# Turning softmax weights by block transposes and a trip through DRAM instead of TensorE transposes, from the tenth head pair on

## The chip, the cores and the metric

One core of a Trainium2 chip runs the kernel. The metric is device time in microseconds (us) of one execution; a version's figure is the median of several runs. One further execution was taken with the profiler, and its rows are what the text argues from.

## The reference

Three parts follow one another, all in float32: sliding-window attention, and two feed-forward layers whose input is the attention's output.

```python
scores = scale * q @ k^T                          # B=4, H=8, S=576, D=64
scores = where((rel >= 0) & (rel < 128), scores - slope_h * |rel|, -1e9)
attn = exp(scores - max); attn = attn / (sum + 1e-9)
x = (attn @ v), heads side by side                # 2304 tokens x 512
h = x @ w_in                                      # 512 x 2048
x = (h * clip(h + 3, 0, 6) / 6) @ w_out
xn = x / sqrt(mean(x*x) + 1e-6) * rms_g
out = (silu(xn @ w_gate) * (xn @ w_val)) @ w_out  # 512 x 1536
```

## The kernel before

The 2304 tokens are 18 tiles of 128, handled in six blocks of three (`BLOCKS`). The program is written out in the order in which each engine is to work; nothing reorders it. Its spine is a row of **slots**. A slot takes one of the 16 chunks of the first layer's hidden width (`m`) for one block: `product1` (L463, 12 matmuls of 384 columns into the single bank `ps_h`), then an activation chain on ScalarE and VectorE that makes `g` from `ps_h` (L699 relu, L700 product, L705 and L711 its high and low part), and `product2` (L476, 9 matmuls of 512 columns) of the slot before, whose `g` is ready. The next slot's `product1` needs `ps_h` free again, which L700 does; `product2` one slot on needs `g`.

Attention is threaded into these slots. A **pair** is two heads of one block: 24 pairs, each of three **steps** (one tile of 128 queries each, against the keys of that tile and the one before). The list `slots` says in which slot each kind of work of a step is done: S scores (L341), the bias, the row's minimum and the exponentials (L355, L362, L370, then the reciprocal on GpSimd, L372 and L373); D the division by the sum (L378); T or L two transposes on TensorE (L384) into the bank `turned_bank`, a copy back to SBUF (L389) and, where the two key tiles were folded into one by a minimum (`joint`, from the tenth pair on), two `affine_select` on GpSimd that unfold them (L391); V the product with the values (L402). From block 2 on a pair begins every four slots, at `m % 4 == 2`, with the plan S (0, 0, 0), D (1, 1, 2), T (-, 2, 3), L (1, -, -), V (5, 5, 5): slots after the pair's first, for its three steps. So the four slots of a cycle are unlike each other: one with the scores, one with the values of the pair before, and two without either.

Beside this run, all issued from one DMA queue (SP) in program order: loads of keys, queries and values (L295, L297, L302); from slot `m = 2` of block 2 on the conversion of the second layer's 36 weight pieces (`Second`: load L202, `begin` and `turn` on VectorE and ScalarE, stores L224 and L230); and `Norm`, which squares, scales and block-transposes three tiles per block (L505, L513, L530) and stores them with four DMAs of 512 runs of 128 bytes each (L520), a run being 32 float32. The last block's 16 slots have no attention, and the second layer follows (L824, L876).

Of the kernel before, what the change touches and what calls it, by code (L numbers as in the profile page):

```python
# [10 lines left out]
F32 = mybir.dt.float32  # L11
# [3 lines left out]
U64 = mybir.dt.uint64  # L15
AF = mybir.ActivationFunctionType
ALU = mybir.AluOpType
# [43 lines left out]
EARLY = {0: 1, 1: 3, 2: 6, 3: 8, M2 - 1: 11}  # L61
PAIRS2 = NTILE // 6

KINDS = "QSDTLV"

OPEN = {"reuse_waits": "tile"}

# [1 line left out]
def f32(ap):  # L69
    return ap.bitcast(F32)  # L70
# [3 lines left out]
def fused_kernel(ctx: ExitStack, tc: tile.TileContext, qd, kd, v, w1, w2, rms_g, out):  # L74
# [113 lines left out]
    class Second:  # L188
# [2 lines left out]

        def __init__(self):
            self.n, self.loaded, self.done, self.raw, self.run = 3 * M2, 0, 0, [], None
            self.whole = [dram.tile([P, 4, HK], F32, tag=f"b_{m}", name=f"b_{m}") for m in range(M2)]
            self.parts = [dram.tile([P, 2, 7, HK], F32, tag=f"t_{m}", name=f"t_{m}") for m in range(M2)]
            self.out = [dram.tile([P, 2, 2, DM], F32, tag=f"w2_{m}", name=f"w2_{m}") for m in range(M2 // 2)]

        def load(self):
            i = self.loaded
            if i < self.n:  # L200
                raw = wcpool.tile([P, DM], U64, tag="w", name="wraw", bufs=2)
                sp.dma_start(out=raw, in_=w2[i // 3, :, (i % 3) * DM : (i % 3 + 1) * DM])  # L202
                self.raw.append(raw)
                self.loaded += 1

        def begin(self):

            if self.raw:
                self.run = convert(self.raw.pop(0), DM, wcpool, 1, 3, vec)
                for _ in range(3):  # L210
                    next(self.run)

        def turn(self):

            if self.run is None:
                return
            i, self.done = self.done, self.done + 1
            m, kind = divmod(i, 3)
            run, self.run = self.run, None
            x = run.send(None)  # L220
            self.load()
            if kind < 2:
                self.begin()
                sp.dma_start(out=self.whole[m][:, kind::2], in_=x.rearrange("p (a k) -> p a k", a=2))  # L224
            else:
                t = wcpool.tile([P, 2, DM], F32R, tag="wt", name="w", bufs=1)
                run.send(t)
                self.begin()
                next(run)
                sp.dma_start(out=self.out[m // 2][:, m % 2], in_=f32(t))  # L230

    class Parts:

# [38 lines left out]
    att = ExitStack()  # L272
    ap = att.enter_context(tc.tile_pool(name="ap", bufs=3))
    xs_of = {}
    pairs_bank = [ps_a.tile([P, 2, 2 * P], F32, tag=f"S{a}", name=f"ps_s{a}") for a in range(2)]
    spare_bank = [ps_out.tile([P, 2 * P], F32, tag=f"o{a}", name=f"ps_s{a}") for a in range(2)]
    turned_bank = ps_a.tile([P, 2, 2, P], F32, tag="T", name="ps_t")
# [3 lines left out]
    class Pair:  # L281
# [25 lines left out]
        def scale(self):  # L307
            q = self.qr[:, : self.n * P]
            vec.tensor_scalar(q, q, qscale[:, self.j : self.j + 1], None, ALU.mult)

        def finish(self):

            nq = self.n * P
            x = self.acc.rearrange("p u q -> p (u q)")[:, :nq]
            if self.j == 0:
                xs = (x0pool if self.b == 0 else xpool).tile([P, KC, 2, 3 * P], F32R, tag="xs", name="xs")
                xs_of[self.b] = [xs[:, c] for c in range(KC)]
            t = xs_of[self.b][self.j]
            act.copy(t[:, 0, :nq], x)
            vec.tensor_sub(t[:, 1, :nq], x, f32(t[:, 0, :nq]))  # L320

    class Step:
# [51 lines left out]

        def divide(self):
            for a in range(2):
                p = self.t[:, a, self.p0 :]
                vec.tensor_scalar(p, p, self.r[:, a : a + 1], None, ALU.mult)  # L378

        def transpose(self):  # L380
            self.ps = turned_bank
            for a in range(2):
                for c in range(self.p0 // P, 2):
                    pe.transpose(self.ps[:, a, c], self.t[:, a, c * P : (c + 1) * P], ident)  # L384

        def weights(self):

            self.pt = ap.tile([P, 2, 2, P], F32, tag="pt", name="pt", bufs=3)
            act.copy(self.pt[:, :, self.p0 // P :], self.ps[:, :, self.p0 // P :])  # L389
            for c, sign in ((0, -1), (1, 1)) if self.joint else ():  # L390
                pool.affine_select(  # L391
                    out=self.pt[:, :, c], in_=self.pt[:, :, 1], compare_op=ALU.is_ge, fill=0.0,
                    base=c - 1, pattern=[[0, 2], [sign, P]], channel_multiplier=-sign,
                )

        def values(self):
            pr = self.pair
            if pr.acc is None:
                pr.acc = sums_bank[:, :3]
            for c in range(self.from_, 2):  # L400
                for a in range(2):
                    pe.matmul(  # L402
                        pr.acc[a * D : (a + 1) * D, self.u],
                        lhsT=pr.vr[:, self.i - 1 + c - pr.lo, a * D : (a + 1) * D],
                        rhs=self.pt[:, a, c],
                        start=(c == self.from_),
                        stop=(c == 1),
                        skip_group_check=True,
                    )
# [8 lines left out]
    for k, pr in enumerate(pairs):  # L418
        b, j = divmod(k, H // 2)
        if b < 2:  # L420
            t0, plan = 3 * j if b == 0 else AHEAD - 3 + 3 * j, {"S": (0, 1, 2), "D": (1, 2, 3), "T": (2, 3, 4), "V": (3, 4, 5)}
        else:
            t0, plan = AHEAD + M1 * (b - 1) - 2 + 4 * j, {"S": (0, 0, 0), "D": (1, 1, 2), "T": (None, 2, 3), "L": (1, None, None), "V": (5, 5, 5)}
        slots["Q"].setdefault(t0 - (2 if b < 2 else 1), []).append(pr)
        for u in range(pr.n):
            step = Step(pr, u)
            for kind, at in plan.items():
                if at[u] is not None:
                    slots[kind].setdefault(t0 + at[u], []).append(step)

# [123 lines left out]
    busy(WARM)  # L554
    pairs[0].scale()
    for t in range(AHEAD):
        q, s_, d_, t_, _, v_ = at(t)
# [104 lines left out]
    for p, (b, m0, m1) in enumerate(PARTS):  # L662
# [13 lines left out]
        xs = xs_of[b]  # L676
        for m in range(m0, m1):
            t, slot = slot, slot + 1
            q, s_, d_, t_, l_, v_ = at(t)
            go = p < 3 or last or (t - AHEAD) % 4 in (0, 3)  # L680
            if p == 3 and m == 2:
                first.close()
                wcpool = second.enter_context(tc.tile_pool(name="wcpool", bufs=1, side="right", **OPEN))
                W2.load()
                W2.load()
# [12 lines left out]
            r = gpool.tile([P, 3 * P], F32, tag="t", name="t", bufs=1)  # L698
            act.activation(r[:, :nq], ps[:, :nq], AF.Relu, bias=three)  # L699
            vec.scalar_tensor_tensor(out=r[:, :nq], in0=r[:, :nq], scalar=6.0, in1=ps[:, :nq], op0=ALU.min, op1=ALU.mult)  # L700
            for x in t_:
                x.weights()
            for x in d_:
                x.divide()
            act.copy(g[:, 0, :nq], r[:, :nq])  # L705
            for x in s_[:2]:
                x.bias()
# [8 lines left out]
            if go:  # L716
                for x in norms:
                    x.scale()
            prepare(q, s_)
            if pend:  # L720
                finish1(go)
            for x in l_:
                x.transpose()
            if p == 0:
                k = m + 1
                W1.load(k + 4)
# [17 lines left out]
            for x in norms:  # L744
                x.store()
            if last:
                if m == 1:
                    fed = Inputs(0)
# [240 lines left out]
```

## Time and profile before

| | |
|---|---|
| median of 3 runs | 943.26 us (942.93 to 944.92) |
| profiled execution | 944.16 us, of which the span in the profile is 942.4 us |
| granted TensorE clock, mean | 0.992 |
| TensorE matmul busy | 924.7 us, 98% |
| VectorE busy | 634.7 us, 67% |
| ScalarE busy | 444.9 us, 47% |
| GpSimd busy | 184.5 us, 20% |
| DMA | 97,242 packets, 175.05 MB |

The engines run side by side, so busy times don't add up. The chain that ended last is followed back from the last instruction: what stands in it set the end. The text below writes slots by their place in a pair's cycle: S slot (`m % 4 == 2`), then V slot, P slot and R slot, `m % 4` being 3, 0 and 1.

### The profile page before, as it was taken

What the parts mean: (1) busy time and instruction counts of PE and PEld (TensorE: products, weight loads), DVE (VectorE), ACT (ScalarE), POOL (GpSimd) and SP (SyncE); (2) the same over time, 40 slices, a digit from 0 to 9 for tenths busy, and PEclk for the clock granted to TensorE, in tenths of its full rate; (3) what the DMA queues carried; (4) which work ended last, traced back from release to release, by engine and by line L of the source; (5) the groups of instructions that cost most, each with busy time, mean ns of one, the idle gap of its engine ahead of it and who ended that gap; (6) DMA issues with size and microseconds to landing.
All of it is one profiled execution on the core that took longest, in us unless ns stands there. A gap on an engine that the chain in (4) does not pass through costs nothing.

```text
span 942.4 us, 14933 instructions
## 1 busy us (share of the span) xinstructions
PE 924.7 (98%) x5474; PEld 818.9 (87%) x5474; DVE 634.7 (67%) x1327; ACT 444.9 (47%) x949; POOL 184.5 (20%) x327
## 2 busy tenths in 40 slices
PE   7899999999999999999999999999999999999998
PEld 4577888888888888888898999999999999999997
DVE  5788667555878777876477567787545577545555
ACT  6899666455555655655455553433131323131120
POOL 4333112333223422422233214110000000000000
PEclk8899999999999999999999999999999999999999
DMA  6455501124776565554356759876757555755521
GB/s 231 177 208 192 193 21 49 34 55 121 200 232 197 164 180 171 178 141 150 123 184 240 290 196 317 288 261 233 253 213 271 202 201 201 268 207 208 208 103 68
DMA packets 97242, 175.05 MB, mean 186 GB/s; under 512 B 42768, under 2 KB 70672, under 8 KB 92816
## 3 DMA queue, kind: packets, MB, share of 16 engines
q1 hardware_dynamic: 97168, 174.09, 54.5%
q8 instruction: 43, 0.70, 0.3%
q14 instruction: 31, 0.25, 0.1%
HBM read 130.03 MB, written 44.04 MB: 185 GB/s over the span
## 4 chain that ended last, share of the span: by engine, by line
PE 85%; DVE 6%; ACT 5%; issue 2%; POOL 1%; DMA 0%; ACTq 0%; POOLq 0%; DVEq 0%
PE ps_o L476 18%; PE ps_h L463 18%; PE ps_y L876 15%; PE ps_o L824 10%; PE ps_S L824 8%; PE ps_A L824 6%; PE ps_h L824 4%; PE ps_av L402 3%; PE ps_t L384 2%; PE ps_s L341 2%; ACT wx L136 1%; DVE t L700 1%; ACT t L370 1%; DVE wx L143 1%; ACT w L145 1%
## 5 line engine op out<-in xcount | busy, mean ns | idle before, releaser
L476 PE MATMUL ps_o<-w,g 128*128 128x512 f32 x864 | 222.0, 401 | 3.3 <-ACT w L145 3.1
L463 PE MATMUL ps_h<-xs,w 128*128 128x384 f32 x1152 | 219.6, 338 | 0.1
L463 PEld LDWEIGHTS ps_h<-xs,w 128*128 128x128 f32 x1152 | 201.9, 188 | 8.6 <-DVE t L700 2.9
L476 PEld LDWEIGHTS ps_o<-w,g 128*128 128x128 f32 x864 | 156.1, 188 | 42.3 <-ACT w L145 5.9
L876 PE MATMUL ps_y<-wo,g 128*128 128x512 f32 (+1 forms) x654 | 150.0, 387 | 0.0
L876 PEld LDWEIGHTS ps_y<-wo,g 128*128 128x128 f32 x654 | 121.9, 188 | 24.0
L700 DVE SCALAR_TENSOR_TENSOR t<-t,ps_h 128x384 f32<-128x384 f32 x96 | 53.2, 554 | 93.8 <-ACT t L699 93.8
L699 ACT ACTIVATE t<-ps_h,three 128x384 f32<-128x384 f32 x96 | 55.3, 576 | 87.7 <-PE ps_h L463 85.6
L884 DVE TENSOR_TENSOR y<-y,ps_y 128x512 f32<-128x512 f32 (+1 forms) x91 | 61.9, 680 | 34.4 <-PE ps_y L876 33.9
L370 ACT ACTIVATE t<-t,m 128x128 f32<-128x128 f32 (+1 forms) x144 | 61.2, 426 | 29.4 <-DVE t L362 16.1
L705 ACT CAST g<-t 128x384 fp32r<-128x384 f32 x96 | 49.3, 514 | 48.7 <-DVE t L700 47.1
L711 DVE TENSOR_TENSOR g<-t,g 128x384 fp32r<-128x384 f32 x96 | 54.7, 570 | 23.0 <-ACT g L705 22.0
L847 ACT ACTIVATE r<-r 128x384 f32<-128x384 f32 x36 | 18.9, 525 | 103.0 <-DVE r L846 103.0
L824 PE MATMUL ps_o<-S,tw 128*128 128x384 f32 x336 | 66.2, 339 | 0.0
L372 POOL TENSOR_SCALAR r<-den 128x2 f32<-128x2 f32 x72 | 27.5, 383 | 185.4 <-ACT t L370 183.7
L824 PEld LDWEIGHTS ps_o<-S,tw 128*128 128x128 f32 x336 | 59.3, 188 | 1.0 <-DVE u L835 0.8
L373 POOL TENSOR_TENSOR r<-r,minus 128x2 f32<-128x2 f32 x72 | 56.0, 777 | 6.0
L391 POOL TENSOR_SCALAR_AFFINE_SELECT pt<-pt 128x256 f32<-128x256 f32 x82 | 34.9, 425 | 95.7 <-ACT pt L389 92.5
L832 ACT COPY s<-ps_S 128x384 f32<-128x384 f32 x18 | 8.6, 479 | 84.0 <-PE ps_S L824 83.9
L136 ACT ACTIVATE wx<-wraw 128x512 f32<-128x512 f32 (+1 forms) x52 | 42.6, 818 | 2.7 <-DMA wraw<-w 2.7
L143 DVE SCALAR_TENSOR_TENSOR wx<-wx,wy 128x512 uint32<-128x512 uint32 (+1 forms) x52 | 43.8, 843 | 0.0
L384 PE MATMUL ps_t<-ident,t 128*128 128x128 f32 x190 | 35.6, 292 | 8.1 <-DVE t L378 6.1
(136 smaller groups left out, 1450.4 us busy)
## 6 DMA issues: line engine op xcount, KB each, us to landing
tw<-t SPq DMA_DIRECT2D x52, 896.0 KB, 6.3
wraw<-w SPq DMA_DIRECT2D x36, 512.0 KB, 4.2
wo<-w SPq DMA_DIRECT2D x18, 1024.0 KB, 4.9
wraw<-w SPq DMA_DIRECT2D x16, 1024.0 KB, 8.5
t<-th SPq DMA_DIRECT2D x12, 896.0 KB, 4.6
t<-tl SPq DMA_DIRECT2D x12, 896.0 KB, 4.5
b<-wx SPq DMA_DIRECT2D x24, 256.0 KB, 3.0
w<-w SPq DMA_DIRECT2D x12, 512.0 KB, 3.2
```

The lines of the kernel that those rows point to most:

```text
L143: vec.scalar_tensor_tensor(out=xi, in0=xi, scalar=3, in1=y, op0=ALU.logical_shift_left, op1=ALU.bitwise_or)
L370: act.activation(p, p, AF.Exp, bias=self.m[:, a : a + 1], scale=-1.0, accum_out=self.den[:, a : a + 1])
L373: pool.tensor_tensor(self.r, self.r, minus, ALU.pow)
L384: pe.transpose(self.ps[:, a, c], self.t[:, a, c * P : (c + 1) * P], ident)
L463: pe.matmul(ps[:, : n * P], lhsT=w[:, a, c * P : (c + 1) * P], rhs=xs[c][:, b, : n * P], start=(k == 0), stop=(k == 3 * KC - 1),)
L476: pe.matmul(o, lhsT=g[:, a, i * P : (i + 1) * P], rhs=w[:, b], start=(m == first and a == 0 and b == 0), stop=(m == last and b == 1),)
L699: act.activation(r[:, :nq], ps[:, :nq], AF.Relu, bias=three)
L700: vec.scalar_tensor_tensor(out=r[:, :nq], in0=r[:, :nq], scalar=6.0, in1=ps[:, :nq], op0=ALU.min, op1=ALU.mult)
L711: vec.tensor_sub(g[:, 1, :nq], r[:, :nq], f32(g[:, 0, :nq]))
L824: pe.matmul(ps, lhsT=w[a][:, k, c * P : (c + 1) * P], rhs=x[:, b, c], start=(start and j == 0), stop=(j == 5), skip_group_check=True,)
L876: pe.matmul(ps[:, cols], lhsT=gs[i + k][:, a, t // 3, t % 3 * P : (t % 3 + 1) * P], rhs=wo[i + k][:, b, cols], start=(k == 0 and a == 0 an ...
L884: vec.tensor_add(acc[t][:, cols], acc[t][:, cols], ps[:, cols])
```

## The change

For the steps of the last 15 pairs (`via`; 45 steps) the weights are turned another way:

- The division moves to ScalarE (two activations with a scale per row, 128x128 each), one slot after the scores, behind `finish1`.
- In the next slot (P) VectorE transposes the step's 128x2x128 weights in blocks of 32x32 (`Step.turn`), and SP stores them to a DRAM tile (`Step.put`, 128 KB, runs of 512 bytes).
- One slot on (R) SP loads the pair's three steps back with four DMAs (`Pair.fetch`, 32 partitions each), which put the blocks at their turned places: 768 runs of 128 bytes per DMA, 3072 per pair.
- One slot on, GpSimd does the `affine_select`s for all three steps (W), and V stays five slots after S.

The 45 TensorE steps of transposing (90 instructions) and their 45 copies from PSUM go. Beyond that: `weights_` is one tile in place of the three `pt` buffers, its axes reordered; stores of converted weights are issued one slot later (`W2.flush`), and those of the norm in the slot after their transposes; a third buffer for the raw weights; the norm's work is done once in four slots (`m % 4 == 1`) rather than twice; and one unit of the first layer's conversion is begun at `m = 5` rather than 7.

```diff
-LAST_UNITS = {CUT: (1, 3, 4), CUT + 1: (4, 5, 7), CUT + 2: (7, 8, 9), CUT + 3: (9, 11, 12)}
+LAST_UNITS = {CUT: (1, 3, 4), CUT + 1: (4, 5, 7), CUT + 2: (5, 8, 9), CUT + 3: (9, 11, 12)}
...
-                raw = wcpool.tile([P, DM], U64, tag="w", name="wraw", bufs=2)
+                raw = wcpool.tile([P, DM], U64, tag="w", name="wraw", bufs=3)
...
+        def flush(self):
+            for out, x in self.stores:
+                sp.dma_start(out=out, in_=x)
+            self.stores = []
...
+        def fetch(self):
+
+            for k in range(0, P, 32):
+                sp.dma_start(
+                    out=weights_[k : k + 32, 1].rearrange("r u a (b s) -> r (u a b) s", s=32),
+                    in_=self.d[:, :, :, k : k + 32].rearrange("u a (b r) s -> r (u a b) s", r=32),
+                )
...
+            self.via = self.joint or self.c0 == P and pair.b * H // 2 + pair.j >= JOINT
+            self.pt = weights_[:, :, u]
...
-                p = self.t[:, a, self.p0 :]
-                vec.tensor_scalar(p, p, self.r[:, a : a + 1], None, ALU.mult)
+                p, r = self.t[:, a, self.p0 :], self.r[:, a : a + 1]
+                if self.via:
+                    act.activation(p, p, AF.Copy, scale=r)
+                else:
+                    vec.tensor_scalar(p, p, r, None, ALU.mult)
+
+        def turn(self):
+
+            vec.transpose(self.t[:, :, :P], self.t[:, :, P:])
+
+        def put(self):
+            if self.first:
+                self.pair.d = dram.tile([3, 2, P, P], F32, tag="pd", name="pd", bufs=2)
+            sp.dma_start(out=self.pair.d[self.u].rearrange("a p k -> p a k"), in_=self.t[:, :, :P])
...
+            steps = {"S": plan["S"], "D": (1, 1, 1), "P": (2, 2, 2), "R": (None, None, 3), "W": (4, 4, 4), "V": (5, 5, 5)} if step.via else plan
...
-            go = p < 3 or last or (t - AHEAD) % 4 in (0, 3)
+            go = p < 3 or last or m % 4 == 1
...
+            for x in w_:
+                x.select()
             ps = ps_h.tile([P, 4 * P], F32, tag="h", name="ps_h")
             product1(ps, W1.w_in(m), xs, n)
...
             vec.scalar_tensor_tensor(out=r[:, :nq], in0=r[:, :nq], scalar=6.0, in1=ps[:, :nq], op0=ALU.min, op1=ALU.mult)
+            for x in p_:
+                x.turn()
             for x in t_:
                 x.weights()
...
             prepare(q, s_)
+            W2.flush()
+            for x in norms:
+                x.store()
+            for x in p_:
+                x.put()
+            for x in r_:
+                x.pair.fetch()
             if pend:
                 finish1(go)
             for x in l_:
                 x.transpose()
+            for x in d_:
+                if x.via:
+                    x.divide()
```

How the instructions move shows in the order of each engine. First TensorE, in the V, P and R slots of a pair from block 2 on, before:

```order
L463 MATMUL ps_h<-xs,w 128x384 x12
L402 MATMUL ps_av<-pt,vraw 64x128 x12
L476 MATMUL ps_o<-w,g 128x512 x9
L384 MATMUL ps_t<-ident,t 128x128 x2
L463 MATMUL ps_h<-xs,w 128x384 x12
L384 MATMUL ps_t<-ident,t 128x128 x2
L476 MATMUL ps_o<-w,g 128x512 x9
L463 MATMUL ps_h<-xs,w 128x384 x12
L384 MATMUL ps_t<-ident,t 128x128 x2
```

and the same stretch of the change (its lines are some 30 higher):

```order
L496 MATMUL ps_h<-xs,w 128x384 x12
L434 MATMUL ps_av<-pt,vraw 64x128 x12
L509 MATMUL ps_o<-w,g 128x512 x9
L496 MATMUL ps_h<-xs,w 128x384 x12
L509 MATMUL ps_o<-w,g 128x512 x9
L496 MATMUL ps_h<-xs,w 128x384 x12
```

The three rows of two transposes are gone, and nothing takes their place on this engine. Second ScalarE, from a V slot to the P slot behind it, in the change:

```order
L734 ACTIVATE t<-ps_h,three 128x384
L743 CAST g<-t 128x384
L335 CAST xs<-ps_av 128x384
L397 ACTIVATE t<-t,r 128x128 x6
L145 CAST w<-wx 128x512
L136 ACTIVATE wx<-wraw 128x512
```

where the kernel before had, between L319 (there the `xs` cast) and the next relu:

```order
L319 CAST xs<-ps_av 128x384
L145 CAST w<-wx 128x512
L136 ACTIVATE wx<-wraw 128x512
L389 COPY pt<-ps_t 128x2x128
L699 ACTIVATE t<-ps_h,three 128x384
```

Six divisions came in ahead of the weight conversion, and the copies left. Third the DMA queue SP, one full cycle of the change from the keys' load in an S slot on:

```order
L303 DMA kraw<-kd 128x512
L305 DMA qraw<-qd 128x384
L216 DMA b_108<-wx 256x1x256
L553 DMA x_0_145<-y 32x16x32 x4
L203 DMA wraw<-w 128x512
L310 DMA vraw<-v 128x4x128
L216 DMA b_108<-wx 256x1x256
L203 DMA wraw<-w 128x512
L216 DMA w_1_130<-w 128x1024
L408 DMA pd<-t 128x2x128 x3
```

Behind them come `L203` (a load), `L216` (the store of the P slot's piece) and the four `L322` that fetch: the three stores of the weights stand behind one store of converted weights, and the fetch behind a load and a store.

## Rows read from the trace of the kernel before

**Rows 1.** The page: span, and part 1, busy time and share of each engine.
```profile
span 942.4 us, 14933 instructions
PE 924.7 (98%) x5474; PEld 818.9 (87%) x5474; DVE 634.7 (67%) x1327; ACT 444.9 (47%) x949; POOL 184.5 (20%) x327
```
**Rows 2.** The chain that ended last, 139 to 445 us: its shares by line.
```profile
by line: PE ps_o L476 39.6%; PE ps_h L463 38.8%; PE ps_av L402 6.0%; PE ps_t L384 3.3%; PE ps_s L341 3.3%; PE ps_t L341 1.3%; DMA wraw<-w 1.1%; DVE t L355 0.9%; ACT t L370 0.8%; DVE t L700 0.7%; ACT t L699 0.7%; issue 0.7%; ACT wx L136 0.6%
```
**Rows 3.** The same chain in time, one pair's cycle: start us, us, what.
```profile
362.18 2.11 PE ps_h L463 x12
...
367.70 2.11 PE ps_h L463 x12
...
373.54 0.22 PE ps_t L384 x2
373.76 2.09 PE ps_h L463 x12
375.85 0.22 PE ps_t L384 x2
376.07 2.06 PE ps_o L476 x9
...
380.24 0.22 PE ps_t L384 x2
...
382.52 2.11 PE ps_h L463 x12
```
**Rows 4.** The same chain, two slots without attention.
```profile
460.37 2.08 PE ps_o L476 x9
462.45 2.10 PE ps_h L463 x12
```
**Rows 5.** TensorE's waits, 139 to 445 us: us in total, times, longest.
```profile
PE ps_t L384 <- ACT pt L389: 0.5, 2, 0.3
```
**Rows 6.** Groups by line and shape: count | busy us, mean ns | idle before, releasers.
```profile
L370 ACT ACTIVATE t<-t,m 128x128 f32<-128x128 f32 x90 | 35.5, 395 | 21.5 <-DVE t L362 16.1 <-POOL r L372 5.5
L389 ACT COPY pt<-ps_t 128x256 f32<-128x256 f32 x45 | 16.4, 365 | 3.8 <-PE ps_t L384 3.6
L378 DVE TENSOR_SCALAR t<-t,r 128x128 f32<-128x128 f32 x98 | 23.0, 289 | 1.6 <-POOL r L373 1.5
L530 DVE STREAM_TRANSPOSE y<-y 128x512 f32<-128x512 f32 x18 | 12.7, 704 | 0.0
L391 POOL TENSOR_SCALAR_AFFINE_SELECT pt<-pt 128x256 f32<-128x256 f32 x82 | 34.9, 425 | 95.7 <-ACT pt L389 92.5
```
**Rows 7.** Timeline of that cycle, ScalarE: V slot into P slot.
```profile
371.89 0.47 ACT L319 CAST xs<-ps_av 128x384 fp32r<-128x384 f32 x1
374.05 0.62 ACT L145 CAST w<-wx 128x512 fp32r<-128x512 f32 x1 [1.69 <-DVE wx L143]
374.58 0.69 ACT L136 ACTIVATE wx<-wraw 128x512 f32<-128x512 f32 x1
...
375.95 0.58 ACT L699 ACTIVATE t<-ps_h,three 128x384 f32<-128x384 f32 x1 [0.42 <-PE ps_h L463]
```
**Rows 8.** The same timeline on GpSimd and VectorE.
```profile
370.77 0.70 POOL L373 TENSOR_TENSOR r<-r,minus 128x2 f32<-128x2 f32 x1
...
376.56 0.56 DVE L700 SCALAR_TENSOR_TENSOR t<-t,ps_h 128x384 f32<-128x384 f32 x1 [1.01 <-ACT t L699]
```
**Rows 9.** DMA from 213.0 to 215.4 us, one tile's four norm stores (128-byte runs).
```profile
DMA packets 2112, 0.26 MB, mean 109 GB/s; under 512 B 2112, under 2 KB 2112, under 8 KB 2112
q1 hardware_dynamic: 2112, 0.26, 68.6%
x<-y SPq DMA_DIRECT2D x3, 64.0 KB, 2.0
```
**Rows 10.** DMA from 169 to 171 us, one load of values (512-byte runs).
```profile
q1 hardware_dynamic: 528, 0.26, 43.6%
```
**Rows 11.** The page, part 6: issues, KB each, median us to landing.
```profile
b<-wx SPq DMA_DIRECT2D x24, 256.0 KB, 3.0
```
**Rows 12.** Busy us (count) of PE, PEld, DVE, ACT, POOL; clock, DMA share, GB/s.
```profile
360.00:380.00 20.00, 20.00 (x137) 17.40 (x137) 15.01 (x41) 11.51 (x31) 5.80 (x13) 1.00 0.50 164
```

More of the change, by code (lines that the diff above doesn't have):

```diff
@@ L62 @@
 PAIRS2 = NTILE // 6
-KINDS = "QSDTLV"
+KINDS = "QSDTLVPRW"
 OPEN = {"reuse_waits": "tile"}
@@ L211, in begin @@
                     next(self.run)
+        def flush(self):
+            for out, x in self.stores:
+                sp.dma_start(out=out, in_=x)
+            self.stores = []
         def turn(self):
@@ L216, in turn @@
                 return
+            self.flush()
             i, self.done = self.done, self.done + 1
@@ L223, in turn @@
                 self.begin()
-                sp.dma_start(out=self.whole[m][:, kind::2], in_=x.rearrange("p (a k) -> p a k", a=2))
+                self.stores.append((self.whole[m][:, kind::2], x.rearrange("p (a k) -> p a k", a=2)))
             else:
@@ L229, in turn @@
                 next(run)
-                sp.dma_start(out=self.out[m // 2][:, m % 2], in_=f32(t))
+                self.stores.append((self.out[m // 2][:, m % 2], f32(t)))
     class Parts:
@@ L274, in fused_kernel @@
     xs_of = {}
+    weights_ = ap.tile([P, 2, 3, 2, P], F32, tag="pt", name="pt", bufs=1)
     pairs_bank = [ps_a.tile([P, 2, 2 * P], F32, tag=f"S{a}", name=f"ps_s{a}") for a in range(2)]
@@ L383, in transpose, with select @@
                 for c in range(self.p0 // P, 2):
-                    pe.transpose(self.ps[:, a, c], self.t[:, a, c * P : (c + 1) * P], ident)
+                    pe.transpose(self.ps[:, c, a], self.t[:, a, c * P : (c + 1) * P], ident)
         def weights(self):
-            self.pt = ap.tile([P, 2, 2, P], F32, tag="pt", name="pt", bufs=3)
-            act.copy(self.pt[:, :, self.p0 // P :], self.ps[:, :, self.p0 // P :])
+            act.copy(self.pt[:, self.p0 // P :], self.ps[:, self.p0 // P :])
+            self.select()
+        def select(self):
             for c, sign in ((0, -1), (1, 1)) if self.joint else ():
                 pool.affine_select(
-                    out=self.pt[:, :, c], in_=self.pt[:, :, 1], compare_op=ALU.is_ge, fill=0.0,
+                    out=self.pt[:, c], in_=self.pt[:, 1], compare_op=ALU.is_ge, fill=0.0,
                     base=c - 1, pattern=[[0, 2], [sign, P]], channel_multiplier=-sign,
@@ L404, in values @@
                         lhsT=pr.vr[:, self.i - 1 + c - pr.lo, a * D : (a + 1) * D],
-                        rhs=self.pt[:, a, c],
+                        rhs=self.pt[:, c, a],
                         start=(c == self.from_),
@@ L426, in fused_kernel @@
             step = Step(pr, u)
-            for kind, at in plan.items():
+            steps = {"S": plan["S"], "D": (1, 1, 1), "P": (2, 2, 2), "R": (None, None, 3), "W": (4, 4, 4), "V": (5, 5, 5)} if step.via else plan
+            for kind, at in steps.items():
                 if at[u] is not None:
@@ L556, in fused_kernel @@
     for t in range(AHEAD):
-        q, s_, d_, t_, _, v_ = at(t)
+        q, s_, d_, t_, _, v_, _, _, _ = at(t)
         scores(s_, t % 2)
@@ L678, in fused_kernel @@
             t, slot = slot, slot + 1
-            q, s_, d_, t_, l_, v_ = at(t)
-            go = p < 3 or last or (t - AHEAD) % 4 in (0, 3)
+            q, s_, d_, t_, l_, v_, p_, r_, w_ = at(t)
+            go = p < 3 or last or m % 4 == 1
             if p == 3 and m == 2:
@@ L683, in fused_kernel @@
                 wcpool = second.enter_context(tc.tile_pool(name="wcpool", bufs=1, side="right", **OPEN))
-                W2.load()
-                W2.load()
+                for _ in range(3):
+                    W2.load()
             for x in late:
@@ L703, in fused_kernel @@
             for x in d_:
-                x.divide()
+                if not x.via:
+                    x.divide()
             act.copy(g[:, 0, :nq], r[:, :nq])
@@ L723, in fused_kernel @@
                 x.transpose()
+            for x in d_:
+                if x.via:
+                    x.divide()
             if p == 0:
@@ L743, in fused_kernel @@
                 W2.turn()
-            for x in norms:
-                x.store()
+            if p < 3 or last:
+                for x in norms:
+                    x.store()
             if last:
```

## The prediction

> **What bounds the kernel now.** I read the engines' busy times first: TensorE is busy for 98% of the span, VectorE for 67%, ScalarE for 47% [rows 1]. The chain that ended last says whether that engine also sets the end where the change sits: from 139 to 445 us, the stretch of the 15 changed pairs, 78% of the chain is the two products L476 and L463, 3.3% the transposes of the weights (L384), and what isn't TensorE adds up to some 5% [rows 2]. In time the chain shows a cycle of four slots of 20.34 us (362.18 to 382.52), with three pieces of 0.22 us of transposes in it, each between two products that lean on it on both sides [rows 3]. Where a slot has none, a product follows the other with no gap: 460.37 + 2.08 = 462.45 [rows 4]. So TensorE runs without pause, and an instruction taken from it shortens the cycle by what it holds there, as long as ScalarE, VectorE, GpSimd and the DMAs keep up. TensorE's clock is granted in full (1.00, the 2.4 GHz level) through the cycle [rows 12], and I expect no change there, as the engine stays as busy.
>
> **Removed from TensorE.** Each of 45 steps loses two transposes. A pair of them holds 0.22 us of the chain, not twice its single duration, since matmuls overlap [rows 3]: 45 x 0.22 = 9.9 us. Cross-check: 3.3% of 306 us is 10.1 us [rows 2]. With them go TensorE's own waits there, 0.5 us, all before a transpose for the copy of the one before [rows 5]. Sum: -10.4 us, all on the path.
>
> **ScalarE.** Out go 45 copies of 365 ns, 16.4 us [rows 6]. In come 90 activations of 128x128. None of that kind is in the trace; the exponential of the same size takes 395 ns [rows 6], an upper bound, and the copy of twice the size 365 ns, from which I take half, 0.18 us, as the lower. I take 0.39, being the row of the same shape: 35 us, so +19 us of ScalarE's time over 300 us. It is busy for 11.5 of 20 us [rows 12], so there is room on average; the place matters. The six stand between the `xs` cast, which ends at 372.36, and the weight conversion. The last reciprocal is there at 371.47 [rows 8], so they run at once: 372.36 + 6 x 0.39 = 374.70, then the two conversions of 0.62 and 0.69 us, until 376.0. The next relu began at 375.95 [rows 7]. It is not delayed by more than 0.1 us, against 0.6 us of room before the next product needs `ps_h` (L700 ends at 377.12 [rows 8]; without the transposes that product is due at 377.7). Cost nothing; with the lower price it would be early.
>
> **VectorE.** Out go 90 divisions of 289 ns, 26 us; in come 45 transposes of 128x256 [rows 6]. The row nearest is the 128x512 transpose of 704 ns; a quarter to all of it bounds them, and I take 0.43 us, somewhat over half for what doesn't shrink with size. 45 x 0.43 = 19 us, so VectorE is relieved by 7 us. They sit behind L700 and ahead of the low part of `g`: 377.12 + 3 x 0.43 = 378.4, then `g` until 379.0, wanted by the R slot's second product at 379.8. At a block's first slot two copies of the sums out of PSUM follow behind this, about 1.3 us, and the next product wants the first of these banks at that same 379.8; at three such boundaries I charge 0.2 us each, 0.6 us.
>
> **The trip through DRAM.** This is what the gain hangs on. The three stores are issued as the transposes end, the last at 378.4. A 64 KB store lands after 2.0 us [rows 9], a 256 KB one after 3.0 [rows 11]; for 128 KB I take the longer, 381.4 (ends: 380.4 and 381.4). The fetch waits on SP for that and moves 3072 runs of 128 bytes. No row shows such a load. The norm's stores have such runs the other way: 68.6% of 16 engines over 2.4 us for 2112 packets is 12.5 ns each [rows 9]. The load of values has runs of 512 bytes in this direction: 43.6% of 16 engines over 2.0 us for 528 is 26.4 ns [rows 10]. Between these two ends the fetch keeps 16 engines busy for 2.4 to 5.1 us. I take the store's price, because the size is the same and a packet's time falls with its size, and stretch it to 3.5 us (3072 / 2112 x 2.4), because those packets needed up to the whole 2.4 us. A 64 KB store of 512 packets takes 0.4 us of that and lands after 2.0, so 1.6 us are fixed: 5.1 us. A store of converted weights stands just ahead of it, some 0.8 us. Landing: 381.4 + 0.8 + 5.1 = 387.3; the ends are 380.4 + 4.0 = 384.4 and 381.4 + 0.8 + 6.7 = 388.9.
>
> **When it has to be there.** The next S slot now begins at 382.52 - 0.66 = 381.86, the next V slot 5.52 us later (367.70 - 362.18 [rows 3]), and its values 2.11 us after that, at 389.49. GpSimd needs two selections of 0.425 us per step first [rows 6]. The third step's values start some 1.0 us behind the first's, so all six, 2.55 us, must be done by 390.5: the fetch has to land by 387.9. It makes this by 0.6 us, with ends at 3.5 us early and 1.0 us late. GpSimd's reciprocals of the next pair stand behind the selections and end at about 393 at the worst, which the divisions behind the V slot's `xs` cast (392) nearly hide. What SP has queued behind the waiting fetch is a load of raw weights, and it now has a third buffer; then keys and queries for two pairs ahead. Nothing there is wanted within 5 us.
>
> **The rest.** The later stores hold SP for the same time as before and shorten its waits; the norm's change moves 0.7 us of transposes out of the P slot, now that the weights' transposes are there. I price these, the third buffer and the earlier unit at nothing: SP and VectorE have idle time to cover them.
>
> **Against the skill.** The row: 128-byte runs, in 32x32 blocks, moved at 12.5 ns a packet [rows 9]. The Trainium skill (VectorE: DVE Perf Modes, section on the three transpose paths) warns that a DMA which transposes by strides is 19 times slower than the crossbar's 1309 ns for 128x128 where the innermost stride at the destination is large; by that, an estimate, a pair's six squares would take about 150 us and the kernel over 2 ms. The rows don't bear this out for runs kept whole, and the kernel's own norm store has the same pattern, so I give that no chance of its own. The Trainium skill (DMA: Bandwidth & Descriptors, Specifications) also names 512 bytes as the least transfer at full rate; the rows agree in bytes (10 against 19 per ns and engine), and the rival below is what this would do here.
>
> **The sum.** Span 942.4 - 10.4 + 0.6 = 932.6 us; the profiled execution has 1.8 us outside it and stood 0.9 us over the median, so the median becomes **933.5 us**.
>
> **Rivals.**
> 1. *The fetch lands late and the values wait.* A wait for GpSimd's selections takes the transposes' place on TensorE, in the V slot. It decides at 387.9. Every 0.1 us beyond costs 15 x 0.1 = 1.5 us; at 0.65 us nothing is left of the gain, and at the upper end, 1.0 us, it is 15 us: 933.5 + 15 = 948.5 us, slower than before. For it: no row shows a load of 128-byte runs, it is as many packets again as the norm stores make in all, and DMA engines are busy at 0.50 already [rows 12]. Against it: the packet price of the same size, and that the other end rests on packets four times as long.
> 2. *The same, by a little:* late by 0.1 to 0.5 us where other transfers collide, on the 12 pairs that run beside the weight conversion: 935 to 941 us.
> 3. *ScalarE becomes the bound in the P slot.* If a division takes 0.5 us or the conversions bunch up, relu and then `ps_h` come late. Room is 0.5 us; a delay of 1.2 us per pair, 0.7 beyond the room, costs 15 x 0.7 = 10.5 us and leaves 943.5 to 944, no change. Against it: the exponential's 395 ns already includes more work than a scaled copy.
>
> **How the numbers follow.** Hidden as worked out, 932 to 935: 0.63. Rival 2: 0.16. Rival 1, beyond 0.65 us: 0.15. Rival 3: 0.06. A measurement of this kernel tells changes of about 0.2% (1.9 us) from none. Faster by more than that takes the first two cases, 0.79; within it fall most of rival 3 and the crossing of rival 1, 0.05; slower 0.16. The range runs from 931.5, with all waits gone and no charge at the boundaries, to 941.0, the end of rival 2.
>
> **What would show it.** Right: the transposes on TensorE count 100 and the cycle in the chain is 19.7 us; the fetch lands within 6 us of its first issue; GpSimd's first selection in the S slot ends its wait on a DMA, and the values (L402's successor) wait for nothing. Wrong: a wait of the values for GpSimd in every cycle (rivals 1 and 2), or of `product1` for L700's successor in the R slot (rival 3).

## The result, and the profile after

The changed kernel takes 934.06 us (median of 4 runs, 933.52 to 934.73); the kernel before took 943.66 us (4 runs, 942.93 to 944.92) on the same chip. The ratio is 0.9897 [0.9882, 0.9912]: faster, against a forecast of 933.5 us with a range from 931.5 to 941.0. The profiled execution took 934.41 us, with a span of 932.7 (forecast 932.6), 9.7 less than before.

The page of the kernel after, its span, busy times and DMA packets; it answers to [rows 1].

```profile
span 932.7 us, 15035 instructions
...
PE 914.9 (98%) x5384; PEld 811.0 (87%) x5384; DVE 636.4 (68%) x1282; ACT 457.4 (49%) x994; POOL 187.2 (20%) x327
...
DMA packets 156522, 186.84 MB, mean 200 GB/s; under 512 B 90528, under 2 KB 129952, under 8 KB 152096
```

TensorE has 90 matmuls and 9.8 us less to do and is still busy for 98%. VectorE is as busy as before (634.7), ScalarE has 12.5 us more. The core moves 59,280 packets more than before for 11.8 MB more: short runs.

The chain that ended last, 139 to 440 us, its shares by line, beside [rows 2]; below it the same chain in time (start us, us, what) for one cycle, beside [rows 3].

```profile
by line: PE ps_o L509 41.8%; PE ps_h L496 41.7%; PE ps_av L434 7.0%; PE ps_s L359 3.9%; PE ps_t L359 1.5%; DVE t L403 0.7%; ACT wx L136 0.4%; DVE wx L143 0.4%; DVE y L530 0.4%; issue 0.4%; DVE t L735 0.3%; ACT t L734 0.3%; DVE g L749 0.3%; 
```
```profile
355.98 2.11 PE ps_h L496 x12
...
363.60 1.46 PE ps_av L434 x24
365.06 2.26 PE ps_o L509 x9
367.33 2.10 PE ps_h L496 x12
369.43 2.08 PE ps_o L509 x9
371.51 2.10 PE ps_h L496 x12
373.62 2.09 PE ps_o L509 x9
375.70 2.12 PE ps_h L496 x12
```

The two products hold 83.5% of the chain now (78.4% before), and the 3.3% of the transposes of weights are gone. The cycle is 375.70 - 355.98 = 19.72 us (20.34 before), and from the values at 363.60 to the next scores each piece ends where the next begins.

The trip through DRAM in that cycle: the timelines of VectorE, SP's queue, GpSimd and TensorE (start us, us, what, idle before and releaser).

```profile
370.61 1.09 DVE L403 STREAM_TRANSPOSE t<-t 128x256 f32<-128x256 f32 x3
```
```profile
371.08 1.46 SPq L408 DMA_DIRECT2D pd<-t  x3
...
373.97 0.53 SPq L216 DMA_DIRECT2D b<-wx  x1
374.68 2.95 SPq L322 DMA_DIRECT2D pt<-pd  x4
```
```profile
380.84 3.01 POOL L423 TENSOR_SCALAR_AFFINE_SELECT pt<-pt 128x256 f32<-128x256 f32 x6 [2.45 <-DMA pt<-pd]
```
```profile
383.26 1.53 PE L434 MATMUL ps_av<-pt,vraw 128*64 128x128 f32 x24
```

The three transposes end at 371.70, the three stores are out at 372.54, the fetch starts at 374.68, GpSimd is released at 380.84, and the values start at 383.26 without a wait. What waits is GpSimd. Its waits and TensorE's, 139 to 440 us (total, times, longest), are these; TensorE's answers to [rows 5].

```profile
POOL pt L423 <- DMA pt<-pd: 122.9, 15, 14.0
```
```profile
PE ps_h L496 <- DVE t L735: 0.6, 1, 0.6
```

The last rows of this section: the new instructions on ScalarE and VectorE by line (min/median/max ns of one), the six divisions of that cycle on ScalarE's timeline with the conversion behind them, the DMA issues (KB each, median us to landing; the last answers to [rows 11]), and the window of one cycle beside [rows 12].

```profile
L397 ACT ACTIVATE t<-t,r x90: 386/390/407, 148.8 to 427.3; 128x128 f32<-128x128 f32 x90
```
```profile
366.44 1.86 ACT L397 ACTIVATE t<-t,r 128x128 f32<-128x128 f32 x6
368.23 0.62 ACT L145 CAST w<-wx 128x512 fp32r<-128x512 f32 x1
```
```profile
L403 DVE STREAM_TRANSPOSE t<-t x45: 401/403/440, 153.4 to 430.5; 128x256 f32<-128x256 f32 x45
```
```profile
b<-wx SPq DMA_DIRECT2D x24, 256.0 KB, 4.4
...
pd<-t SPq DMA_DIRECT2D x45, 128.0 KB, 2.0
pt<-pd SPq DMA_DIRECT2D x60, 96.0 KB, 4.0
```
```profile
360.00:380.00 20.00, 20.00 (x135) 17.39 (x134) 16.19 (x41) 13.75 (x37) 8.13 (x16) 1.00 0.84 216
```

The DMA engines go from 0.50 to 0.84 busy in this window for 216 in place of 164 GB/s, and a store of converted weights lands after 4.4 us in place of 3.0. TensorE's clock stays at 1.00.

Where the time went can be read slot by slot, a slot's length being the difference of the starts of two successive first products (`ps_h`) on TensorE's timeline, in us. The first four rows are the most frequent lengths; in some cycles S and V are 0.1 to 0.2 us shorter, in both kernels alike:

| slot | before | after |
|---|---|---|
| S | 5.51 | 5.51 |
| V | 5.98 | 5.83 |
| P | 4.46 | 4.19 |
| R | 4.40 | 4.19 |
| the P slots of 291.46, 332.62 and 414.23 us before | 4.92, 4.67, 4.92 | 4.19 each |
| the four last-block slots that begin at 491.65 us before | 4.26, 4.27, 4.41, 4.28 | 4.19, 4.19, 4.19, 4.30 |
| the R slots of 271.67 and 292.04 us after | 4.40, 4.39 | 4.95, 4.54 |

A cycle gains 0.15 + 0.27 + 0.21 = 0.63 us, 15 cycles 9.45. The three long P slots gave 0.46 + 0.21 + 0.46 = 1.1 us on top, and slots that were little longer than their kind 0.2. Lost, measured against their kind, are 0.76 and 0.35 us in the two R slots and 0.1 to 0.2 in each of four others, 1.6 in all. At the end of attention the kernel is thus 9.1 us ahead, and the four last-block slots add 0.35: 9.45 of the span's 9.7 us, the rest below what this reading resolves.

### The profile page after: what moved, and what is told of

Its sections match the earlier page's. It is cut to its first block, busy times and chain, and to the rows that moved or that the text cites. A ratio compares the mean times of both kernels' runs of the same rounds, so it can differ in the third digit from the quotient of the medians.

```text
span 932.7 us, 15035 instructions
## 1 busy us (share of the span) xinstructions
PE 914.9 (98%) x5384; PEld 811.0 (87%) x5384; DVE 636.4 (68%) x1282; ACT 457.4 (49%) x994; POOL 187.2 (20%) x327
## 4 chain that ended last, share of the span: by engine, by line
PE 89%; DVE 5%; ACT 4%; issue 1%; POOL 1%; ACTq 0%; POOLq 0%; DVEq 0%
PE ps_o L509 20%; PE ps_h L496 19%; PE ps_y L925 15%; PE ps_o L873 10%; PE ps_S L873 8%; PE ps_A L873 6%; PE ps_h L873 4%; PE ps_av L434 3%; PE ps_s L359 2%; ACT wx L136 1%; DVE wx L143 1%; ACT w L145 1%; PE ps_t L414 1%; ACT t L388 1%; DVE t L735 1%
## 5 line engine op out<-in xcount | busy, mean ns | idle before, releaser
L509 PE MATMUL ps_o<-w,g 128*128 128x512 f32 x864 | 219.8, 398 | 3.3 <-ACT w L145 3.1
L734 ACT ACTIVATE t<-ps_h,three 128x384 f32<-128x384 f32 x96 | 55.2, 576 | 67.9 <-PE ps_h L496 62.2
L749 DVE TENSOR_TENSOR g<-t,g 128x384 fp32r<-128x384 f32 x96 | 56.2, 586 | 21.0 <-ACT g L743 20.9
L423 POOL TENSOR_SCALAR_AFFINE_SELECT pt<-pt 128x256 f32<-128x256 f32 x82 | 38.2, 481 | 125.7 <-DMA pt<-pd 122.9
L391 POOL TENSOR_TENSOR r<-r,minus 128x2 f32<-128x2 f32 x72 | 54.1, 751 | 6.0
L136 ACT ACTIVATE wx<-wraw 128x512 f32<-128x512 f32 (+1 forms) x52 | 42.4, 815 | 0.9 <-DVE w L147 0.9
L434 PE MATMUL ps_av<-pt,vraw 128*64 128x128 f32 x544 | 40.0, 287 | 0.3 <-DVE xs L336 0.2
```

What stands on the lines that cost most here:

```text
L391: pool.tensor_tensor(self.r, self.r, minus, ALU.pow)
L434: pe.matmul(pr.acc[a * D : (a + 1) * D, self.u], lhsT=pr.vr[:, self.i - 1 + c - pr.lo, a * D : (a + 1) * D], rhs=self.pt[:, c, a], start=( ...
L509: pe.matmul(o, lhsT=g[:, a, i * P : (i + 1) * P], rhs=w[:, b], start=(m == first and a == 0 and b == 0), stop=(m == last and b == 1),)
L749: vec.tensor_sub(g[:, 1, :nq], r[:, :nq], f32(g[:, 0, :nq]))
```

## The experiments

My theory (A in the expectations): the gain is TensorE's transposes alone, the edits beside them are worth nothing by themselves, and the fetch and ScalarE fit with some 0.5 us to spare each. Rivals: the gain is from the later stores; or the fit has much more, or no, room. Each difference below is to the change, each of the two taken against its own runs of the kernel before (the change: 943.66 - 934.06 = 9.60 us faster).

**The side edits alone.** Later stores, third buffer, earlier unit and the norm's slot stay; no pair takes the new way.

```diff
-            self.via = self.joint or self.c0 == P and pair.b * H // 2 + pair.j >= JOINT
+            self.via = False
```

> The side edits alone (norm once in four slots, later stores, third raw buffer, earlier conversion unit), with the weights still transposed on TensorE and divided on VectorE as before. Theory A (the gain is the 45 x 0.22 us that the transposes held on TensorE, the rest is hidden): no gain, 943 to 945 us. Rival B (a good part of the gain is the rearranged stores and norm): 941 us or less.

Measured: 943.53 us, ratio 1.0003 [0.9994, 1.0013], no difference that can be measured. Slot by slot they do move something: of the three long P slots of before, the second and third read 4.46 in this kernel, and the first 5.24 in place of 4.92.

**The new way alone.** The opposite: the side edits undone.

```diff
-LAST_UNITS = {CUT: (1, 3, 4), CUT + 1: (4, 5, 7), CUT + 2: (5, 8, 9), CUT + 3: (9, 11, 12)}
+LAST_UNITS = {CUT: (1, 3, 4), CUT + 1: (4, 5, 7), CUT + 2: (7, 8, 9), CUT + 3: (9, 11, 12)}
...
-raw = wcpool.tile([P, DM], U64, tag="w", name="wraw", bufs=3)
+raw = wcpool.tile([P, DM], U64, tag="w", name="wraw", bufs=2)
...
-self.stores.append((self.whole[m][:, kind::2], x.rearrange("p (a k) -> p a k", a=2)))
+sp.dma_start(out=self.whole[m][:, kind::2], in_=x.rearrange("p (a k) -> p a k", a=2))
...
-go = p < 3 or last or m % 4 == 1
+go = p < 3 or last or (t - AHEAD) % 4 in (0, 3)
...
-            for x in norms:
-                x.store()
...
-                if p < 3 or last:
-                    for x in norms:
-                        x.store()
+                for x in norms:
+                    x.store()
```

> The new way of turning the weights alone, with stores, norm, raw buffers and conversion unit where they stood before. Theory A says that the fetch has about 0.5 us to spare; the norm's four stores of 512 runs now stand ahead of the fetch on the queue in two of four pairs, some 3 us of queue time, so the values wait there: 936 to 946 us. If the side edits do nothing (the fetch has 3 us or more to spare): 933.5 to 935.

Measured: 944.92 us, ratio 1.0015 [1.0005, 1.0024]. The whole gain is lost, 11.0 us. SP's queue in one cycle of this kernel, and TensorE's values behind it:

```profile
255.56 1.70 SPq L408 DMA_DIRECT2D pd<-t  x3
...
258.79 2.79 SPq L553 DMA_DIRECT2D x<-y  x4
261.70 2.16 SPq L322 DMA_DIRECT2D pt<-pd  x4
```
```profile
266.87 0.44 PE L434 MATMUL ps_av<-pt,vraw 128*64 128x128 f32 x4 [1.01 <-DMA pt<-pd]
```

The same cycle of the change:

```profile
251.99 1.45 SPq L408 DMA_DIRECT2D pd<-t  x3
...
255.77 2.71 SPq L322 DMA_DIRECT2D pt<-pd  x4
...
261.18 3.57 SPq L553 DMA_DIRECT2D x<-y  x4
```

From the end of the stores to the fetch it is 261.70 - 257.26 = 4.4 us in place of 255.77 - 253.44 = 2.3, because the norm's four stores hold SP for 2.8 us ahead of it; in the change they are issued behind it. The values come late, and this V slot takes 7.78 us in place of 5.62; two more of the 15 lose over 2 us, two some 0.8. Another 0.8 us is lost where the first layer's conversion has its unit back at `m = 7`: the P slot that begins at 149.71 us, and the R slot behind it, take 4.88 and 4.30 us, 4.19 each in the change. ScalarE's timeline shows why: the unit's L131 and L136 stand between the divisions and relu (L734), which in the change follows L145 directly.

```profile
151.30 1.14 ACT L131 ACTIVATE wy<-wraw 128x1024 uint32<-128x1024 uint32 x1
152.34 1.14 ACT L136 ACTIVATE wx<-wraw 128x1024 f32<-128x1024 f32 x1
153.39 0.56 ACT L734 ACTIVATE t<-ps_h,three 128x384 f32<-128x384 f32 x1
```

**Which of the side edits.** First only the norm's slots and stores undone (the last three pieces of the diff above), then only the stores of converted weights and the third buffer.

> The change, with only the norm's slots and the place of its stores as before; converted weights still stored a slot later, three raw buffers. Theory A: the norm's four stores ahead of the fetch are what made the version without the side edits wait, so nearly all of its loss is here: 941 to 946 us. If the later stores of converted weights were what mattered: 934 to 937.

Measured: 939.29 us, ratio 0.9954 [0.9939, 0.9969], 5.1 us lost, less than expected. Five V slots take 0.6 to 2.1 us longer.

> The change, with the converted weights stored in the slot of their conversion and two raw buffers as before; the norm as in the change. Theory A: little, 933.5 to 936.5 us. If these stores, which wait for VectorE at the queue's head, hold the fetch back: 940 or more.

Measured: 934.74 us, ratio 0.9904 [0.9889, 0.9919], 0.5 us lost, no difference that can be measured. The two don't add up to the 11.0 of both together. The earlier unit, which both these versions keep, is 0.8 us of the difference: the P slot in question reads 4.19 in both. Most of the rest is in two V slots, which begin at 341.61 and 420.50 us in the change: undoing the norm costs them 0.8 us and nothing, undoing the other stores costs neither anything, and undoing both costs 2.2 and 2.4. That fits a fetch that stands behind both kinds of stores, where what the first takes of the spare time the second can no longer use.

**The transposes put back as dead weight.** The new way stays, and TensorE does two transposes per step, of a constant, at the places of before.

```diff
+        def idle(self):
+            for a in range(2):
+                pe.transpose(turned_bank[:, 1, a], ident, ident)
...
+            for x in x_:
+                x.idle()
...
```

> The change, with two transposes of the identity per step put back on TensorE where the removed ones stood; nothing reads them. Theory A: their price is 45 x 0.22 = 9.9 us, so 943.5 to 944.5 us. If TensorE has gaps there in which they hide, or the gain has another source: under 938.

Measured: 942.36 us, ratio 0.9987 [0.9978, 0.9997]: 8.4 us of the 9.6 are given back, a little less than expected. Two pieces of its chain, in the cycle that begins at 361 us:

```profile
372.85 0.22 PE ps_t L418 x2
...
375.17 0.22 PE ps_t L418 x2
```

The V, P and R slots read 5.97, 4.46 and 4.38 again, those of before, so the regular cycles give back all that they had gained. The three P slots that were long before stay at 4.46, the last-block slots at 4.19, and the R slot that the change made 4.95 reads 4.53. So the instructions are worth the gain of the regular cycles, and waits that this kernel lacks as the change does make up the difference.

**How late the fetch may be.** One extra DMA of 768 runs ahead of each fetch, into the half of the tile that the selections write afterwards; then four, with `range(0, 128, 32)` (768 and 3072 runs).

```diff
+            for k in range(0, 32, 32):
+                sp.dma_start(
+                    out=weights_[k : k + 32, 0].rearrange("r u a (b s) -> r (u a b) s", s=32),
+                    in_=self.d[:, :, :, k : k + 32].rearrange("u a (b r) s -> r (u a b) s", r=32),
+                )
```

> The change, with one more DMA of 768 runs of 128 bytes ahead of each fetch, into the half of the tile that the selections overwrite. It lands the fetch about 0.9 us later. Theory A (0.5 us to spare, then 15 us per us): 0.2 to 0.6 us late per pair, 937 to 943 us. If the fetch has 1 us or more to spare: 934 to 935.

Measured: 937.01 us, ratio 0.9932 [0.9917, 0.9947], 3.1 us lost. GpSimd is released some 0.7 us later where no conversion runs beside the fetch, and 0.3 to 1.9 later where it does. Five V slots are 0.2 to 0.6 us longer; counted from the start of the slot, their release comes 0.9 to 2.0 us later than in the change, so 0.7 to 1.4 us were spare in them.

> The change, with the whole fetch issued a second time ahead of the real one, into the half that the selections overwrite: 3072 more runs of 128 bytes. They need some 3.5 us of the DMA engines. Theory A (the spare is used up by one extra DMA of 768 runs, and every us beyond costs 15 us): 2.3 to 3.2 us late per pair, 968 to 985 us. If something else gives way, such as the load that stands behind: under 955.

Measured: 962.65 us, ratio 1.0200 [1.0180, 1.0220], 28.4 us lost, less than expected. TensorE's weight loads in it, 135 to 460 us:

```profile
PEld ps_av L439 <- POOL pt L428: 24.4, 67, 1.5
```

Where no conversion runs beside it, the time from the fetch's first issue to GpSimd's release goes from 4.7 to 7.7 us. The first such cycle, in the change and here (the profile puts the wait here down to a load of keys issued just behind the fetch; the last of the fetch lands 0.2 us ahead of the release in both):

```profile
157.32 2.04 SPq L322 DMA_DIRECT2D pt<-pd  x4
```
```profile
162.00 2.63 POOL L423 TENSOR_SCALAR_AFFINE_SELECT pt<-pt 128x256 f32<-128x256 f32 x6 [13.99 <-DMA pt<-pd]
```
```profile
158.08 2.04 SPq L322 DMA_DIRECT2D pt<-pd  x4
```
```profile
165.74 2.62 POOL L428 TENSOR_SCALAR_AFFINE_SELECT pt<-pt 128x256 f32<-128x256 f32 x6 [17.44 <-DMA kraw<-kd]
```

So 3072 runs take 3.0 us, or 15.6 ns each on one of 16 engines. At the prediction's price, 28.4 / 15 = 1.9 us per pair are lost, so on average 3.0 - 1.9 = 1.1 us were spare, in line with the 0.7 to 1.4 above. Single V slots lose from nothing to 4.4 us.

**How late ScalarE may be.** The divisions back on VectorE, in the new place; then each of them on ScalarE followed by a copy of the same size.

```diff
-                if self.via:
-                    act.activation(p, p, AF.Copy, scale=r)
-                else:
-                    vec.tensor_scalar(p, p, r, None, ALU.mult)
+                vec.tensor_scalar(p, p, r, None, ALU.mult)
```

> The change, with the six divisions on VectorE instead of ScalarE, at the same place in the slot. Theory A (both engines have room on average, but the chain from ps_h through the transposes to the fetch runs over VectorE there): relu is early but VectorE's product of the P slot comes up to 1 us late, and with it the transposes and the fetch: 935 to 941 us. If the engine makes no difference: 933.5 to 934.7.

Measured: 939.10 us, ratio 0.9955 [0.9941, 0.9969], 5.1 us lost (the change beside it on this chip: 933.96 against 943.21, 9.25 faster). The waits of TensorE's weight loads, 135 to 460 us:

```profile
PEld ps_h L493 <- DVE t L732: 7.6, 12, 1.6
```

The time was as expected, and VectorE's product (L732, behind relu) is late as expected. What waits is another: the next first product for `ps_h`, which L732 frees (1.8 us in three waits in the change), while every V slot keeps its length, so the fetch is not late for the values.

```diff
                     act.activation(p, p, AF.Copy, scale=r)
+                    act.activation(p, p, AF.Copy)
```

> The change, with each division followed by a copy of the same size on ScalarE, six more activations of 0.39 us per pair. Rival 3 of the prediction put ScalarE's room there at 0.5 us: then 2.0 us less 0.5 at a price of 15 us per us, 945 to 962 us. If ScalarE has room for it: 934 to 937.

Measured: 952.22 us, ratio 1.0093 [1.0072, 1.0113], 18.3 us lost. TensorE's waits, 135 to 460 us:

```profile
PE ps_h L497 <- DVE t L736: 13.2, 14, 1.9
```

The P slot goes from 4.19 to between 5.1 and 5.6 us in nine of 15 cycles; the others lose 0.1 to 0.6, one 2.1. From the first division to the conversion behind the last it is 152.87 - 149.04 = 3.83 us in the first pair here, and 150.57 - 148.80 = 1.77 in the change, so the six copies add 2.1 us. At 15 us per us, 18.3 / 15 = 1.2 are lost: on average some 0.8 us were free. This is rival 3's mechanism, at a price that the change doesn't reach.

**The lost R slot.** The chain of the change at 271 us, where it leaves TensorE:

```profile
271.14 1.09 DVE t L403 x3
...
274.13 0.68 DVE w L147
...
274.84 0.67 ACT wx L136
275.51 0.48 ACT t L734
...
276.01 0.57 DVE t L735
...
276.62 2.36 PE ps_h L496 x12
```

The three block transposes push back the conversion on VectorE. ScalarE's L136, which begins the next weight piece, waits 0.91 us for L147, the last operation of this one; and relu, L734, stands behind L136 although its input was ready at 273.8. So `ps_h` is 0.6 us late. If that is the cause, beginning the next piece ahead of that last stage frees ScalarE:

```diff
-                run.send(t)
                 self.begin()
+                run.send(t)
```

> The change, with the next piece's conversion begun ahead of the last stage of the piece before it, so that ScalarE's read of the raw weights (line 136) no longer stands behind that stage. Theory A (the one slot of 4.95 us in the change is ScalarE held for VectorE's subtraction): that slot goes back to 4.2 us, 933.0 to 933.8 us. If the slot is long for another reason: 934 to 934.6, and the slot stays.

Measured: 933.32 us, ratio 0.9889 [0.9873, 0.9906]. The same stretch of its chain:

```profile
271.97 2.10 PE ps_h L496 x12
274.07 2.08 PE ps_o L509 x9
276.16 2.11 PE ps_h L496 x12
```

Both R slots are back at 4.19, so the mechanism is shown for the first. The second, at 292.04, is the first R slot of a block, and the chain of the change runs there over other work, the two copies out of PSUM (L530) among it:

```profile
293.33 1.20 DVE y L530 x2
...
296.09 0.44 DVE t L735
...
296.57 2.38 PE ps_h L496 x12
```

With the conversion begun first the same two copies stand there, 0.5 us earlier in the cycle, and cost nothing. So the copies alone don't make this slot long; that the delay of the slots before adds to them is argued, not shown. One V slot elsewhere grew by 0.26 us. To measure its worth, this version and the change ran again side by side.

> The change itself, once more, so that the version with the conversion begun first is compared with it on one chip: 933.5 to 934.7 us.

> The change with the next piece's conversion begun first, once more on the same chip: 0.5 to 1.2 us under the change (its one slot of 4.95 us at 4.19, two slots behind it back to their length). If the first look was noise: within 0.3 us of it.

Measured: the change 933.96 us (933.26 to 934.53; 0.9899 [0.9884, 0.9913]), the version 932.93 (932.14 to 933.52; 0.9888 [0.9873, 0.9902]). It is 1.0 us better in this pair and 0.9 in the first; the ranges overlap slightly, so its lead over the change is likely rather than certain, while it beats the kernel before clearly.

## Why the prediction was right

**TensorE: 45 x 0.22 = 9.9 us.** Right in kind: the regular cycles gain 9.45 us, and putting the transposes back costs 8.4. The price by the chain held, 0.21 us per step (0.63 / 3); the count by a transpose's own duration, 90 x 0.273 (L414's median in the profile after), would have given 24.6 us.

**The waits, 0.5 us.** Too small. [rows 5] names only TensorE's idle time before a transpose. The three long P slots, the slightly longer ones and the last block's show that 1.1 + 0.2 + 0.35, some 1.65 us, went away; the last block's I hadn't charged at all. Not all of it is the transposes': two of the long P slots go with the side edits alone, by 0.21 and 0.46 us. The last block's waits are there with the side edits alone (4.28, 4.29, 4.39, 4.30) and gone with the dead transposes put back, so they go with the new way; why is open, as that block has no attention.

**ScalarE.** One division lasts 390 ns, as taken from the exponential. Six in a row, though, hold the engine for 368.23 - 366.44 = 1.8 us, not 6 x 0.39 = 2.3: they overlap, as the transposes on TensorE do, and I asked only there for the time held. So ScalarE's busy time grew by 12.5 us and not by 19. The error was on the safe side. The room left beyond the divisions, given as 0.5 to 0.6 us, is some 0.8 on average.

**VectorE and the boundaries: +0.6 us.** The transpose took 403 ns (taken: 430). The relief of 7 us in busy time didn't come; the sum never used it. The divisions had held the engine for 23.0 us in all 98, 0.235 each and not their mean of 289 ns [rows 6], and the fold (L362, now L380) takes 20.0 us in place of 16.9. The boundaries, charged with 0.6 us, cost 0.16 at 213.30, where a weight load of the second product waits 0.34 us for a copy out of PSUM (0.19 before), 0.35 at 292.04, whose chain is shown above, and nothing at 371.35: 0.5 us, about right, though the larger part goes with the conversion begun first and so isn't the copies' alone.

```profile
215.94 1.46 PEld L509 LDWEIGHTS ps_o<-w,g 128*128 128x128 f32 x7 [0.34 <-DVE y L526]
```

What the sum lacked is the other 1.1 us of the 1.6 lost, 0.76 of it in the R slot at 271.67: ScalarE's L136, held by a conversion that the transposes delay, with relu behind it. I had looked at ScalarE's order in a regular cycle [rows 7] and not in one where a piece of three stages ends. That the total came out as forecast is in part luck, as the errors nearly cancel: 9.45 + 1.65 - 1.6 = 9.5 against 9.9 + 0.5 - 0.6 = 9.8.

**The trip.** From the transposes' end to the landing I had put 387.3 - 378.4 = 8.9 us; in the cycle shown GpSimd is released 380.84 - 371.70 = 9.1 us after it. This too is in part luck, as its two parts err in opposite ways. The fetch begins 374.68 - 371.70 = 3.0 us after the transposes and not 3.8, because a 128 KB store lands after 2.0 us and not 3.0, and the store of converted weights that I had put behind that landing goes out while the three stores land. From its first issue the fetch then takes 6.2 us and not 5.1. Across cycles this is 4.6 to 4.7 us in the four without conversion beside it, 5.0 in the one where the conversion's loads begin, and 5.5 to 6.7 in the ten with it; in nine of the 15 it is over 6, so this sign of being right did not come. The others did: 100 transposes on TensorE (L414), the cycle of 19.72 us, GpSimd's wait ending on a DMA and the values without a wait. The time of one run, 15.6 ns, lies between the two ends, nearer to the store's 12.5 [rows 9]; that it is slower beside the conversion, by some 1.5 us, is rival 2's mechanism, and the spare time took it up. From the release to the values it is 2.4 us where 2.2 were forecast. The spare time, 0.6 us in the prediction, is 1.1 on average.

**Rivals 1 and 2** were mechanisms that exist (the fetches make 15 x 3072 = 46,080 runs, a quarter more than the norm stores' 18 x 2048 = 36,864): a fetch later by 3.0 us loses 28.4, which fits 15 us per us beyond a spare of 1.1. The change stays on the good side of that point.

**"I price these at nothing"**, said of the later stores and the norm's slots: right as an addition to before, and wrong as a reading of the change; the earlier unit, priced at nothing too, is worth 0.8 us in it. Without the later stores the fetch stands behind the norm's stores on SP and the gain is gone. I had listed what SP has queued behind the fetch; ahead of it I counted only one store, 0.8 us, without seeing that it is the edit itself which keeps the other four out.

**The skill.** The Trainium skill (VectorE: DVE Perf Modes, the three transpose paths) gave, by its factor of 19 on a crossbar time that it has for bfloat16, an estimate of 150 us per pair; this fetch was done within 6.7 us at the longest. The warning has a condition, a large innermost stride at the destination, which this fetch doesn't meet: its runs are 32 neighbouring elements at both ends. The Trainium skill (DMA: Bandwidth & Descriptors, Specifications) names 512 bytes as the least transfer at full rate, and the runs agree: 128 / 15.6 = 8.2 bytes per ns and engine, against 19 for 512-byte runs [rows 10]. No size between the two was run, so where the full rate begins is not shown.

## What to carry to other kernels

Price an instruction by the time that it holds its engine and not by how long it lasts, and then ask what the replacement waits for; here both are small numbers, 0.22 us per step and 1.1 us of spare time per pair. When data takes a detour through DRAM on a shared queue, what is issued ahead of the load decides whether it fits: an edit that is worth nothing alone can be what makes the other one pay. And read the order of every engine in the unusual cycles too, since that is where the rest of the gain was lost.

## What the runs showed of the hardware that was not expected

The DMA engines' share in the cycle rose from 0.50 to 0.84 for a third more bytes, and the stores of converted weights landed 1.4 us later, while none of TensorE's waits names them. VectorE's fold by a minimum, whose input and shape didn't change, took 487 ns on average (L380 after) against 412 (L362 before), and the low part of `g` 587 (L749) against 559 (L711), both from 139 us to the end of attention, and the slowest selection on GpSimd 723 against a median of 410; what they met there is open. Delays on one queue were not additive: two V slots that lost 0.8 and nothing with one kind of store ahead of the fetch, and nothing with the other, lost 2.2 and 2.4 us with both.
